# Starting a transform's first stage before the transform ahead of it has ended

## The chip, the cores and the metric

The kernel runs on one core of a Trainium2 chip. The metric is the device time of one execution in microseconds (us), the median of several runs. A core has TensorE (matmuls; PE in the profile, with its weight loads as PEld), VectorE (DVE), ScalarE (ACT), GpSimd (POOL) and SyncE (SP), which only issues DMAs here. Each engine works through its own queue in order.

## The reference

For each of 8 batches of 3008 tokens x 256 channels: a real Fourier transform along the tokens, a product with a filter, the transform back. All 24064 tokens then go through an MLP with a hidden size of 2048. All arrays are float32.

```python
X = np.fft.rfft(x, axis=1)
Y = X * (filt_r + 1j * filt_i)[None]
y = np.fft.irfft(Y, n=S, axis=1)          # (8, 3008, 256)
h = y.reshape(B * S, D) @ w_in            # 256 -> 2048
g = h * (1.0 / (1.0 + np.exp(-1.702 * h)))
out = g @ w_out                           # 2048 -> 256
```

## The kernel before

**The MLP** sets the order of everything. The tokens are cut into 48 tiles (six for each batch) of 512 columns, or 384 for the sixth tile of an even batch. Each tile has 16 **chunks** of 128 hidden units, so the main loop over `turns` has 768 chunks, numbered 0 to 767. A chunk is twelve matmuls: six into `h` (line 784; operands are split into a high and a low part, and three products are kept), ScalarE's Gelu into `gh` (line 787) and again in place (line 788), VectorE's difference `gl` (line 789), and six matmuls into `o` (line 808). From chunk 96 the first half of a chunk is traced two chunks ahead of its second half.

**The transform of a batch** (`fft(b)`) is a generator that the main loop advances by a step now and then. A length of 3008 is split into 64 x 47. From the third batch on (b = 2, `packed`), the **first stage** has 24 steps `transform(n, h)`: POOL's sums and differences of the two halves of `x` (line 519), a split by ScalarE and POOL (lines 525 and 526), one matmul (line 537), a copy by ScalarE and two sums by VectorE (lines 539 to 541), and a store to `a_d` in device memory, issued by ScalarE two steps later (line 468). Four steps that load the first of `x` and prepare the first operands come ahead. The **second stage** has 64 steps (two halves of `forward(i)` and two of `backward(i)`, i from 0 to 15): POOL loads `zy` from `a_d` (line 574), matmuls multiply by the 47-point matrices (lines 585 to 588; those of i = 0 by lines 585 and 586), VectorE and POOL multiply by the filter (lines 596 to 617), and the results go to `b_d`. The tiles' own preparation (`signal`, `turned_signal`) reads `b_d` later.

**When a step is taken** is written out by hand. Each batch but the first has a leg, a list of costs (`COSTS`); the main loop takes the next step when the chunks passed since the leg before have reached its share. Legs follow each other: batch b's first step comes when the last step of batch b - 1 has been taken. A leg ends 18 chunks (12 in one case) ahead of the tile that needs it.

**The order in the queues** is not simply the order of the program. The Tile framework is called with `schedule_with_timeline_sim=True`: it orders each engine's instructions by the times at which it expects their operands. Matmuls marked `keep_in_program_order` (those of the transform among them) keep their order among such instructions.

**Buffers.** In the first stage `x`, the results `a` (two steps to a buffer) and later also `be`, `br` and `zt` share one ring, `raw`, of seven buffers; the split operands, the sums `ev` and the tiles' halves share `half`, of seven. `b_t`, a tile of 24 KB a partition, is used by the first batch alone.

Of the kernel before, what the change touches and what calls it, by code (L numbers as in the profile page):

```python
# [20 lines left out]
P = 128  # L21
Q = 112
NFC = DFF // P
LATER = [0.5, 0.5, 1.0, 0.4] + [0.625, 0.625, 0.375, 0.375] * 15 + [1.0]
COSTS = [[0.746] * 12 + [1.212] * 2 + LATER] + [[0.8] * 4 + [0.675] * 24 + [1.3] * 2 + LATER] * 7

LEAST = 2.0**-15
MOST = float(np.uint32(0x47EFFFFF).view(np.float32))
# [139 lines left out]
def tile_kernel(  # L168
# [19 lines left out]
    def raw(name):  # L188
        return sb.tile([P, 4, D], F32, tag="raw", name=name, bufs=7)
# [270 lines left out]
    def fft(b):  # L460
# [4 lines left out]
        def keep(n=2):  # L465

            for pair in late[:n]:
                nc.scalar.dma_start(*pair)
            del late[:n]

        def thrice():

            for c in range(6):
                xr = raw(f"x_{b}_{c}")
                load_in(xr, x[b, c])
                ah, al = (sb.tile([P, 4, D], F32R, tag="raw", name=f"a{n}_{b}_{c}", bufs=7) for n in "hl")
                for u in range(2):
                    xh, xl = half(f"xh_{b}_{c}_{u}"), half(f"xl_{b}_{c}_{u}")
                    src = xr[:, 2 * u : 2 * u + 2, :]
                    nc.scalar.copy(xh, src)  # L480
                    nc.gpsimd.tensor_tensor(xl, src, xh.bitcast(F32), ALU.subtract)
                    ps = ring("f", [P, 2, D], f"s1_{b}_{c}_{u}")
                    mm3(ps, t1_sb[0][:, 0], t1_sb[0][:, 1], xh, xl)
                    su = slice(2 * u, 2 * u + 2)
                    nc.scalar.copy(ah[:, su], ps)
                    nc.vector.tensor_tensor(al[:, su], ps, ah[:, su].bitcast(F32), ALU.subtract)
                    keep()
                    yield
                for k, a in enumerate((ah, al)):
                    for j in range(2):  # L490
                        n = NH * j + 4 * c
                        pair = (a_d[k][:, n : n + 4], a[64 * j : 64 * j + 64].bitcast(F32))
                        if b == 1:
                            late.append(pair)
                        else:
                            nc.scalar.dma_start(*pair)

        def packed():

            if b == 2:  # L500
                t1_sb.append(const.tile([P, 2, 2, 2, 64], F32R, tag="t1_sb", name="t1_two"))
                t1 = table["t1_s"].rearrange("p (a c) -> p a c", a=2)
                for h in range(2):
                    hi = t1_sb[1][:, h, :, h]
                    nc.scalar.copy(hi, t1)
                    nc.vector.tensor_tensor(t1_sb[1][:, h, :, 1 - h], t1, hi.bitcast(F32), ALU.subtract)
            sides = [(slice(64 * h, 64 * h + 64), slice(64 - 64 * h, P - 64 * h)) for h in range(2)]
            xs, sums, es = {}, {}, {}

            def fetch(c):  # L510
                if c < 6:
                    xs[c] = raw(f"x_{b}_{c}").rearrange("p (j i) d -> p j i d", j=2)
                    load_in(xs[c], x[b, c].rearrange("p (j i) d -> p j i d", j=2))

            def butterfly(n):
                if n < 12:
                    c, j = divmod(n, 2)
                    sums[n] = xs[c][:, 1] if j else sb.tile([P, 2, D], F32, tag="half", name=f"ev_{b}_{c}", bufs=7)
                    nc.gpsimd.tensor_tensor(sums[n], xs[c][:, 0], xs[c][:, 1], ALU.subtract if j else ALU.add)

            def split(n, h):
                if n < 12:
                    src, (t, o) = sums[n], sides[h]
                    es[n, h] = half(f"e{h}_{b}_{n}")
                    nc.scalar.copy(es[n, h][t], src[t])
                    nc.gpsimd.tensor_tensor(es[n, h][o], src[t], es[n, h][t].bitcast(F32), ALU.subtract)

            made = {}

            def transform(n, h):  # L530
                c, j = divmod(n, 2)
                if h == 0:
                    made[n] = sb.tile([P, 2, 2, D], F32, tag="raw", name=f"a_{b}_{n}", bufs=7)
                a, (t, o) = made[n], sides[h]
                ps = ring("f", [P, 2, D], f"s1_{b}_{n}_{h}")
                w = t1_sb[1][:, h, j].rearrange("p a c -> p (a c)")
                tc.keep_in_program_order(nc.tensor.matmul(ps, w, es.pop((n, h)), start=True, stop=True))  # L537
                hi, lo = a[t, 0].bitcast(F32R), a[t, 1]
                nc.scalar.copy(hi, ps[t])  # L539
                nc.vector.tensor_tensor(lo, ps[t], a[t, 0], ALU.subtract)  # L540
                nc.vector.tensor_tensor(lo.bitcast(F32R), lo, ps[o], ALU.add)
                q = NH * j + 4 * c + 2 * h
                late.append((a_d[:, :, q : q + 2].rearrange("k s n d -> s k n d"), a[t]))

            for c in range(2):
                fetch(c)
            for c in range(2):
                yield
            butterfly(0)
            butterfly(1)  # L550
            yield
            for h in range(2):
                split(0, h)
            yield
            for n in range(12):
                for h in range(2):
                    transform(n, h)
                    split(n + 1, h)
                    if h:
                        butterfly(n + 2)  # L560
                        if n % 2 == 0:
                            fetch(n // 2 + 2)
                    if len(late) > 2:
                        keep(1)
                    yield

        yield from packed() if b > 1 else thrice()

        b_d = dram.tile([48, 64, D], F32, tag="b_d", name=f"b_d{b}")

# [5 lines left out]
        def load_f(i):  # L576
            for k in range(2):
                load_in(f_buf[64 * k : 64 * k + 48, 2 * (i % 2) : 2 * (i % 2) + 2], fs[i])
# [54 lines left out]
                        nc.scalar.dma_start(b_d[:, 32 * n + 4 * g : 32 * n + 4 * g + 4, :], be[64 * n : 64 * n + 48])  # L633
                yield

        keep(4)
        if b == 1:
            nc.gpsimd.memset(zy[0].bitcast(F32), 0.0)
        for i in range(2):
            load(i)  # L640
            load_f(i)

        for i in range(2):
            yield
        for i in range(17):
            if i < 16:
                yield from forward(i)
            if i:
                yield from backward(i - 1)
        b_of[b] = b_d  # L650

    def signal(b, t, y):

# [181 lines left out]

    carry = const.tile([P, 2, 2, 64], F32R, tag="carry", name="carry")
    b_t = []
    ys, t2_two, gelu = {}, [], []

    def start(b, t):  # L840
        ys[b, t] = sb.tile([P, 2, 2, 512], F32R, tag="y", name=f"y_{b}_{t}")
# [32 lines left out]
    for j in range(2, len(tiles)):  # L874
# [5 lines left out]
            steps = [NFC * (j - 1) + k for k in at]  # L880
        for n in steps:
            due.setdefault(n, []).append(j)
    legs, passed, since = [], 0, 0
    for b in range(B - 1):
        upto = sum(NFC * width(i) for i in range(6 * b + 6)) - 4 * LEAD - ((18 if b > 1 else 12) * width(6 * b + 5) if b else 26)
        legs.append((COSTS[b], list(COSTS[b]), upto))
    nxt = [fft(1)]
    for n, (i, fc) in enumerate(turns):
        b, t = tiles[i]
        if n == 0:  # L890
            run(start(*tiles[1]))
        if n == 2 * NFC:
            shared[0] = "f"
        if n == 6 * NFC:
            shared[0] = "h"
        while begun <= min(n + 1 + (n >= 6 * NFC), len(turns) - 1):
            ahead(*turns[begun])
            begun += 1
        chunks_of[i][1](fc, turns[n + 1 : n + 2] == [(i, fc + 1)])
        if fc == 1:  # L900
            store()
        if n < 26:
            run(conv, 1)
            if n % 2 and n < 12:
                load_unit(EARLY + 9 + n // 2)
        if n == 11:
            split_de()
            in_order[0] = False
        if n == 26:
            zy.append(const.tile([P, 4, 2, 2, D], F32R, tag="zy", name="zy"))  # L910
        if n >= LEAD and legs:
            passed += width(i)
            costs, steps, upto = legs[0]
            while steps and sum(costs) - sum(steps) + steps[0] <= sum(costs) * (passed - since) / (upto - since) + 0.01:
                run(nxt[0], 1)
                steps.pop(0)
            if not steps:
                legs.pop(0)
                nxt[0] = fft(B - len(legs)) if legs else None
                since = upto  # L920
        for j in due.pop(n, ()):
            if j not in sigs:
                sigs[j] = start(*tiles[j])
            run(sigs[j], 1)
            if not any(j in later for later in due.values()):
                run(sigs[j])
# [29 lines left out]
```

## Time and profile before

| what | value |
|---|---|
| median of 3 runs | 2334.66 us (2334.61 to 2335.33) |
| the profiled execution's own time | 2334.13 us |
| its span, first to last instruction | 2332.3 us |
| busy: TensorE / VectorE / ScalarE / POOL | 100% / 69% / 62% / 48% |
| HBM read and written | 173.80 and 114.82 MB |

The time is taken around the execution; the span is read from the trace of one such execution and lies inside it. Busy is the share of the span in which an engine has an instruction under way; the ends of matmuls are modelled.

### The profile page before, as it was taken

The numbers are of one execution on the slowest core, as the hardware profiler recorded it, in microseconds if no ns is written. First come the engines' busy times: TensorE is split into PE (matmuls) and PEld (weight loads), VectorE is DVE, ScalarE is ACT, GpSimd is POOL, SyncE is SP. The second block draws the span as 40 slices with busy tenths as digits, with TensorE's granted clock in tenths as the row PEclk, the third lists the DMA queues.
The fourth block names the chain that finished last, engine by engine and source line by source line (L and its number), as shares of the span: only waits on it lengthen the run. The fifth ranks groups of instructions, "written<-read, shape, count | busy, mean of one in ns | idle before, by whom it ended". The sixth has DMA issues, their size and how long they took to land.

```text
span 2332.3 us, 32211 instructions
## 1 busy us (share of the span) xinstructions
PE 2324.5 (100%) x10630; PEld 1944.9 (83%) x10630; DVE 1607.8 (69%) x2404; ACT 1439.8 (62%) x2654; POOL 1128.0 (48%) x999
## 2 busy tenths in 40 slices
PE   9999999999999999999999999999999999999999
PEld 7878898888888889888888888988888888888887
DVE  7978866688667885678855887568876688623222
ACT  6666657666675666756676666766657666544443
POOL 3035546466564665556654565736657466311010
PEclk9999999999999999999999999999999999999999
DMA  9265545566455664556545554555655465411100
GB/s 338 82 192 111 111 107 146 134 135 135 109 145 125 144 140 127 154 121 139 127 133 141 133 128 117 153 134 125 138 134 145 118 138 118 101 52 52 57 28 19
DMA packets 189238, 290.75 MB, mean 125 GB/s; under 512 B 18576, under 2 KB 125200, under 8 KB 189072
## 3 DMA queue, kind: packets, MB, share of 16 engines
q1 hardware_dynamic: 112368, 178.20, 26.5%
q0 software_dynamic: 46592, 44.05, 11.4%
q10 hardware_dynamic: 30112, 66.44, 11.1%
q8 instruction: 85, 1.39, 0.3%
q14 instruction: 81, 0.66, 0.1%
HBM read 173.80 MB, written 114.82 MB: 124 GB/s over the span
## 4 chain that ended last, share of the span: by engine, by line
PE 93%; DVE 0%; ACT 0%; issue 0%
PE o L808 42%; PE h L784 42%; PE s L588 2%; PE i L588 2%; PE s L537 1%; PE i L305 1%; PE i L307 1%; PE i L306 1%; PE i L700 0%; PE bt L671 0%; PE s L585 0%; PE s L586 0%; PE i L586 0%; PE i L585 0%; DVE out L816 0%; ACT gh L787 0%
## 5 line engine op out<-in xcount | busy, mean ns | idle before, releaser
L784 PE MATMUL h<-y,wi 128*128 128x512 f32 (+1 forms) x4608 | 1177.3, 385 | 0.1
L784 PEld LDWEIGHTS h<-y,wi 128*128 128x128 f32 x4608 | 858.9, 188 | 165.2 <-DVE gl L789 1.0
L789 DVE TENSOR_TENSOR gl<-h,gh 128x512 fp32r<-128x512 f32 (+1 forms) x768 | 520.7, 678 | 495.4 <-ACT h L788 467.9
L808 PE MATMUL o<-gh,wo 128*128 128x512 f32 (+1 forms) x3072 | 839.2, 385 | 1.2 <-ACT gh L787 1.2
L787 ACT ACTIVATE gh<-h 128x512 fp32r<-128x512 f32 (+1 forms) x768 | 452.2, 589 | 606.6 <-PE h L784 462.9
L808 PEld LDWEIGHTS o<-gh,wo 128*128 128x128 f32 x3072 | 573.4, 188 | 111.6 <-ACT gh L787 1.9
L808 PE MATMUL o<-gl,wo 128*128 128x512 f32 (+1 forms) x1536 | 481.6, 385 | 0.5 <-DVE gl L789 0.5
L788 ACT ACTIVATE h<-h 128x512 f32<-128x512 f32 (+1 forms) x768 | 449.0, 585 | 0.0
L617 POOL TENSOR_TENSOR zy<-c_buf,zy 48x512 fp32r<-48x512 f32 x224 | 316.0, 1411 | 75.0 <-DVE zy L616 63.3
L808 PEld LDWEIGHTS o<-gl,wo 128*128 128x128 f32 x1536 | 287.5, 188 | 56.5 <-DVE gl L789 1.1
L612 POOL TENSOR_TENSOR c_buf<-c_buf,u_buf 112x512 f32<-112x512 f32 x112 | 144.6, 1291 | 229.2 <-DVE c_buf L611 229.2
L574 POOL DMA_DIRECT2D zy<-a_d x224 | 130.3, 586 | 232.5 <-PE s L588 92.9
L740 POOL TENSOR_TENSOR bl<-br,bh 128x512 fp32r<-128x512 f32 x80 | 107.1, 1353 | 246.5 <-ACT bh L739 204.7
L720 POOL TENSOR_TENSOR y<-y 128x512 fp32r<-128x512 f32 (+1 forms) x86 | 105.3, 1230 | 205.2 <-ACT y L719 193.8
L597 DVE TENSOR_TENSOR c_buf<-s,c_buf 48x512 f32<-48x512 f32 x224 | 154.1, 688 | 33.3 <-ACT c_buf L596 28.6
L596 ACT COPY c_buf<-s 48x512 f32<-48x512 f32 x224 | 130.2, 581 | 70.9 <-PE s L588 58.5
L596 ACT COPY b<-i 48x512 f32<-48x512 f32 x224 | 130.1, 581 | 58.4 <-PE i L588 46.5
L597 DVE TENSOR_TENSOR b<-i,b 48x512 f32<-48x512 f32 x224 | 153.8, 687 | 15.1 <-ACT b L596 10.3
L540 DVE TENSOR_TENSOR a<-s,a 64x512 f32<-64x512 f32 x144 | 99.0, 688 | 63.3 <-ACT a L539 60.5
L616 DVE CAST zy<-c_buf 48x512 fp32r<-48x512 f32 x224 | 109.4, 488 | 39.8 <-POOL c_buf L612 34.6
L605 DVE TENSOR_TENSOR u_buf<-c_buf,f_buf 48x512 f32<-48x512 f32 x112 | 110.3, 985 | 3.8
L539 ACT CAST a<-s 64x512 fp32r<-64x512 f32 x144 | 83.7, 581 | 40.8 <-PE s L537 26.6
(126 smaller groups left out, 1789.5 us busy)
## 6 DMA issues: line engine op xcount, KB each, us to landing
f_buf<-fs SPq DMA_DIRECT2D x224, 192.0 KB, 3.4
zy<-a_d POOLq DMA_DIRECT2D x224, 192.0 KB, 3.7
a_d<-a ACTq DMA_DIRECT2D x144, 256.0 KB, 3.0
x<-in_x_dram SPq DMA_DIRECT2D x47, 512.0 KB, 5.5
out_dram<-out SPq DMA_DIRECT2D x43, 512.0 KB, 3.7
b_d<-b ACTq DMA_DIRECT2D x112, 192.0 KB, 2.8
br<-b_d SPq DMA_DIRECT2D x84, 256.0 KB, 4.5
z_d<-zt SPq DMA_DIRECT2D x40, 512.0 KB, 2.7
```

What stands on the lines that cost most here:

```text
L574: nc.gpsimd.dma_start(zy[0][64 * k : 64 * k + 48, i % 2].rearrange("p k s d -> p (k s) d"), src)
L596: nc.scalar.copy(dst[h], ps[o])
L597: nc.vector.tensor_tensor(dst[h], ps[h], dst[h], ALU.add)
L605: nc.vector.tensor_tensor(u2[64:Q], u1[0:48], f_i[0:48], ALU.mult)
L612: nc.gpsimd.tensor_tensor(u1, u1, u2, ALU.add)
L616: nc.vector.tensor_copy(y[h, k], u1[h])
L617: nc.gpsimd.tensor_tensor(y[o, k], u1[h], y[h, k].bitcast(F32), ALU.subtract)
L784: nc.tensor.matmul(ps[:, :w], wi_sb[half][:, wk, kc, c], y[:, yk, kc, :w], start=n == 0, stop=n == 5)
L787: nc.scalar.activation(gh[:, :w], ps[:, :w], AF.Gelu_apprx_sigmoid)
L788: gelu.append(nc.scalar.activation(ps[:, :w], ps[:, :w], AF.Gelu_apprx_sigmoid).ins)
L789: nc.vector.tensor_tensor(gl[:, :w], ps[:, :w], gh[:, :w].bitcast(F32), ALU.subtract)
L808: ins = nc.tensor.matmul(pos[m][:, :w], wb[:, P * m : P * m + P], g[:, :w], start=first_one, stop=last_one)
```

## The change

The generator `fft` becomes a function that returns two generators, the first stage and `two()`, the second. Each step of both gets a time of its own, in sixteenths of a tile's columns passed, and all steps of all batches are sorted into one list. `SPACED` gives, for the third, the fourth and all later batches: how many chunks ahead of the end of the transform in hand the first stage begins (0, 16, 24), how many of its 24 steps lie there (0, 4, 6, one in four chunks), and over how many chunks after that end the others are spread (26, 20, 17). The four preparing steps lie 6, 4.5, 2.2 and 1.1 chunks ahead of the first. The loads of `zy` come 1.5 chunks after the last first-stage step and the first second-stage step 4 chunks after it; the rest of the second stage is spread over what is left, up to the same end as before.

The first stage's buffers become one tile, `s1_pool`, in the memory of `b_t`: three places for `x`, two for the results `a`, and one for two `ev`. The transform of b = 1 (`thrice`) keeps its times.

```diff
-COSTS = [[0.746] * 12 + [1.212] * 2 + LATER] + [[0.8] * 4 + [0.675] * 24 + [1.3] * 2 + LATER] * 7
+SPACED = [(0, 0, 26), (16, 4, 20), (24, 6, 17)]
+FIRST_LEG = [0.746] * 12 + [1.212] * 2 + LATER
...
             if b == 2:
+                s1_pool.append(const.tile([P, 6, 4, D], F32, tag="b_t", name="s1_pool"))
...
-                    xs[c] = raw(f"x_{b}_{c}").rearrange("p (j i) d -> p j i d", j=2)
+                    xs[c] = s1_pool[0][:, c % 3].rearrange("p (j i) d -> p j i d", j=2)
...
-                    sums[n] = xs[c][:, 1] if j else sb.tile([P, 2, D], F32, tag="half", name=f"ev_{b}_{c}", bufs=7)
+                    sums[n] = xs[c][:, 1] if j else s1_pool[0][:, 5, 2 * (c % 2) : 2 * (c % 2) + 2]
...
-                    made[n] = sb.tile([P, 2, 2, D], F32, tag="raw", name=f"a_{b}_{n}", bufs=7)
+                    made[n] = s1_pool[0][:, 3 + n % 2].rearrange("p (k u) d -> p k u d", k=2)
...
-        yield from packed() if b > 1 else thrice()
+        def two():
+            keep(len(late))
...
+            b_of[b] = b_d
...
+        return packed() if b > 1 else thrice(), two()
...
+            early, beside, alone = SPACED[min(b, 4) - 2]
+            first = since - 4 * early
+            last = since + 4 * alone
+            lead = first - 4 * np.array([6.0, 4.5, 2.2, 1.1])
+            one = [*lead, *(first + (since - first) * np.arange(beside) / max(beside, 1))]
+            one += list(since + (last - since) * (np.arange(24 - beside) / (23 - beside)))
+            two = [last + 4 * 1.5, last + 4 * 3, *(last + 4 * 4 + (upto - last - 4 * 4) * np.cumsum([0.0, *LATER[1:]]) / sum(LATER[1:]))]
+        one = [*one, two[0]]
+        steps += [(when, b, which) for which, ats in enumerate((one, two)) for when in ats]
+        since = upto
+    steps.sort()
...
-        if n >= LEAD and legs:
+        if n >= LEAD:
             passed += width(i)
...
+            while steps and steps[0][0] <= passed + 0.01:
+                _, leg, which = steps.pop(0)
+                if leg not in legs:
+                    legs[leg] = fft(leg)
+                run(legs[leg][which], 1)
```

## Rows read from the trace of the kernel before

**Rows 1.** The page: span, and TensorE's busy time, share and instructions

```profile
span 2332.3 us, 32211 instructions
PE 2324.5 (100%) x10630; PEld 1944.9 (83%) x10630; DVE 1607.8 (69%) x2404; ACT 1439.8 (62%) x2654; POOL 1128.0 (48%) x999
```

**Rows 2.** Windows, TensorE alone: stretch, us, busy (matmuls), granted clock, DMA share, GB/s

```profile
0.00:175.00 175.00, 171.58 (x886) 1.00 0.62 204
175.00:2325.00 2150.00, 2150.00 (x9734) 1.00 0.49 118
2325.00:2332.30 7.30, 2.88 (x13) 0.96 0.19 72
```

**Rows 3.** Waits of TensorE: for whom, us in total, times, longest

```profile
PE o L808 <- ACT gh L787: 1.2, 2, 1.0
PE idle L326 <- DVE zero L373: 1.1, 1, 1.1
```

**Rows 4.** Windows: busy (count) of PE, PEld, DVE, ACT, POOL, then clock, DMA

```profile
757.90:816.20 58.30, 58.30 (x259) 48.30 (x258) 52.30 (x78) 37.32 (x68) 35.22 (x34) 1.00 0.68 144
...
2098.80:2157.10 58.30, 58.30 (x259) 48.28 (x258) 17.89 (x26) 26.09 (x48) 7.66 (x6) 1.00 0.17 51
```

**Rows 5.** Waits of ScalarE and POOL, columns as in rows 3

```profile
ACT gh L787 <- PE h L784: 462.9, 455, 4.2
...
POOL zy L574 <- PE s L588: 92.9, 44, 6.0
```

**Rows 6.** Timeline: one Gelu, and the matmuls that read its result

```profile
1560.09 0.60 ACT L787 ACTIVATE gh<-h 128x512 fp32r<-128x512 f32 x1 [1.48 <-PE h L784]
...
1565.78 1.07 PE L808 MATMUL o<-gh,wo 128*128 128x512 f32 x4
```

**Rows 7.** Windows by stage, columns as in rows 4

```profile
709.00:906.00 197.00, 197.00 (x897) 166.05 (x896) 155.53 (x226) 121.71 (x227) 111.19 (x105) 1.00 0.57 129
906.00:988.00 82.00, 82.00 (x384) 70.59 (x383) 54.90 (x82) 59.87 (x112) 51.38 (x40) 1.00 0.57 160
...
334.20:350.90 16.70, 16.70 (x104) 16.70 (x104) 5.54 (x10) 7.72 (x18) 1.08 (x1) 1.00 0.37 87
```

**Rows 8.** Source views of lines 468 and 574: durations in ns, landing times

```profile
L468 ACTq DMA_DIRECT2D a_d<-a x144: 581/582/646, 357.9 to 1836.0; - x144
...
DMA to landing us min/median/max: 2.9/3.1/7.2
...
L574 POOL DMA_DIRECT2D zy<-a_d x224: 574/582/730, 171.6 to 1993.7; - x112
...
DMA to landing us min/median/max: 3.1/3.7/7.1
```

**Rows 9.** Timeline at the fourth batch's handover: start, us, instruction, idle before it

```profile
987.60 0.39 PE L537 MATMUL s<-e,t_two 128*128 128x512 f32 x1
...
990.13 0.58 ACTq L468 DMA_DIRECT2D a_d<-a  x1
...
993.65 2.29 POOL L574 DMA_DIRECT2D zy<-a_d  x4 [16.38 <-DMA a_d<-a]
...
1000.30 0.28 PE L585 MATMUL s<-zy,de_sb 128*128 128x256 f32 x1
...
1000.76 0.28 PE L585 MATMUL s<-zy,de_sb 128*128 128x256 f32 x1
```

**Rows 10.** Timeline at the third batch's handover

```profile
708.26 0.39 PE L537 MATMUL s<-e,t_two 128*128 128x512 f32 x1
...
717.26 2.29 POOL L574 DMA_DIRECT2D zy<-a_d  x4 [16.16 <-issue]
...
721.80 0.19 PEld L585 LDWEIGHTS s<-zy,de_sb 128*128 128x128 f32 x1 [0.21 <-issue]
721.86 0.33 PE L585 MATMUL s<-zy,de_sb 128*128 128x256 f32 x1
```

**Rows 11.** Source view of line 605: durations of one shape, min/median/max in ns

```profile
L605 DVE TENSOR_TENSOR u_buf<-c_buf,f_buf x112: 684/860/1814, 182.2 to 2009.1; 48x512 f32<-48x512 f32 x112
```

More of the change, by code (lines that the diff above doesn't have):

```diff
@@ L565, in packed @@
                     yield
-        yield from packed() if b > 1 else thrice()
+        def two():
+            keep(len(late))
+            if b == 1:
+                nc.gpsimd.memset(zy[0].bitcast(F32), 0.0)
+            for i in range(2):
+                load(i)
+                load_f(i)
+            for i in range(2):
+                yield
+            for i in range(17):
+                if i < 16:
+                    yield from forward(i)
+                if i:
+                    yield from backward(i - 1)
+            b_of[b] = b_d
         b_d = dram.tile([48, 64, D], F32, tag="b_d", name=f"b_d{b}")
@@ L634, in backward @@
                 yield
[L636 to L650, printed above, removed]
+        return packed() if b > 1 else thrice(), two()
     def signal(b, t, y):
@@ L837, in tile_kernel @@
     b_t = []
-    ys, t2_two, gelu = {}, [], []
+    ys, t2_two, gelu, s1_pool = {}, [], [], []
     def start(b, t):
@@ L882, in tile_kernel @@
             due.setdefault(n, []).append(j)
[L883 to L887, printed above, removed]
+    steps, passed, since = [], 0, 0
+    for b in range(1, B):
+        upto = sum(NFC * width(i) for i in range(6 * b)) - 4 * LEAD - ((18 if b > 2 else 12) * width(6 * b - 1) if b > 1 else 26)
+        if b == 1:
+            at = np.cumsum(FIRST_LEG) * (upto / sum(FIRST_LEG))
+            one, two = at[:12], at[12:]
+        else:
+            early, beside, alone = SPACED[min(b, 4) - 2]
[9 more added lines that the diff above has]
+    steps.sort()
+    legs = {}
     for n, (i, fc) in enumerate(turns):
@@ L910, in tile_kernel @@
             zy.append(const.tile([P, 4, 2, 2, D], F32R, tag="zy", name="zy"))
-        if n >= LEAD and legs:
+        if n >= LEAD:
             passed += width(i)
[L913 to L920, printed above, removed]
+            while steps and steps[0][0] <= passed + 0.01:
[3 more added lines that the diff above has]
+                run(legs[leg][which], 1)
         for j in due.pop(n, ()):
```

## The prediction

> **What bounds the kernel now.** I read the page first: the span is 2332.3 us and TensorE is busy for 2324.5 of them [rows 1]. The profiled execution as a whole took 2334.13 us, so 1.8 us lie around the span; the median of the runs shown, 2334.66, is 0.5 us above that execution. Next I cut TensorE's time into three stretches [rows 2]: from 175 to 2325 us it is busy for 2150.00 of 2150.00 us. All its idle time is 3.4 us before 175 (set-up and first transform) and 4.4 us in the last 7.3 (the last outputs). The waits of TensorE say the same: the longest entry is 1.2 us in the whole run [rows 3].
>
> A modelled busy time could hide waiting, so I counted matmuls. The stretch 757.9 to 816.2 lies in a second stage, with the transform's work on every engine; 2098.8 to 2157.1 comes after all transforms. Both hold 259 matmuls in 58.3 us [rows 4], 0.225 us for each, although VectorE is busy for 52.3 us in the first and 17.9 us in the second. The granted clock is 1.00 in both, the level of 2.4 GHz. So TensorE issues at a fixed rate whatever the transform does beside it. A chunk (twelve MLP matmuls) is 12 x 0.225 = 2.70 us. The kernel's time is its number of matmuls times that pace.
>
> What the transform must not do is to make TensorE wait. ScalarE waits for TensorE, not the other way round: 455 of the 768 first Gelus found ScalarE idle until the matmul was done, 462.9 us in total [rows 5]. The Gelu of 1560.09 ends at 1560.69; counting on, the matmuls that read its result are those of 1565.78 [rows 6], 5.1 us later. A delay of ScalarE under some 5 us is not felt there.
>
> **The change part by part.**
>
> *Counts.* No matmul, cast, subtraction or DMA is added or removed: 0 us. One tile of six blocks takes the place of buffers from the shared rings, in memory whose last reader (the first transform's last turn, at chunk 73) lies before its first use at chunk 79. The program of the first transform is the same but for one generator split in two at the same chunk.
>
> *The second stage has more room* (from 58 to 79 chunks for 64 steps: 1.10 to 0.81 steps a chunk, and 0.25 first-stage steps a chunk come in beside it at its end). Any gain would have to come out of TensorE's waiting, and after 175 us there is none that the view shows: 0 us. The most that could be saved at all is the 7.8 us outside the busy time, and the change touches neither end.
>
> *The first stage, 24 steps.* Per step I take the stage 906 to 988 [rows 7] less the load of a stretch with no transform [rows 4], scaled by 82/58.3: ScalarE (59.87 - 36.70)/24 = 0.97 us, VectorE (54.90 - 25.16)/24 = 1.24, POOL (51.38 - 10.77)/24 = 1.69. The steps after the second stage's end came one per 1.17 chunks, now about one per 1.05. With one chunk and one matmul, 2.93 us, for a step, the loads become: ScalarE 45% + 0.97/2.93 = 78%, VectorE 31% + 42% = 73%, POOL 13% + 58% = 71%. Nobody fills up; the cover is the 5 us of [rows 6], the price 0. For the second batch the stage begins 10 chunks earlier, in the narrow tile. In 334 to 351 us, ScalarE is busy 46%, VectorE 33%, POOL 6% [rows 7]; six steps add 5.8, 7.4 and 10.1 us to the 7.7, 5.5 and 1.1 there, below the 16.7 + 1.4 us of the stretch: 0.
>
> *The steps beside the second stage* (four or six, one in four chunks). Their 6 x 1.69 = 10.1 us on POOL stand behind the loads of zy there, which wait at POOL's head for a matmul, up to 6.0 us at a time [rows 5]. A step's operands are split two steps ahead, now eight chunks or 21.6 us, so 6 us don't reach TensorE. The six x loads of a batch go out earlier on SP, past the filter's and the signal's loads; a slot is free four steps before its load, so SP's queue isn't held: 0.
>
> *Slots.* The results of the first stage have two buffers instead of a share of seven. A step writes where the step four before it wrote; that store is issued two steps later, so it has two steps, 5.9 us, to land. Stores land in 3.1 us in the median and 7.2 at most [rows 8]: typically no wait, at worst 1.3 us of ScalarE, with the Gelus behind it, inside the 5 us. Value 0; the other end is a rival below.
>
> *The handover, the only place where something gets tighter.* After the last first-stage matmul: copy and sums, the last store, its landing, the loads of zy by POOL, their landing, then the first second-stage matmul. In the fourth batch the matmul of 987.60 is followed by the last store at 990.13 and four zy loads from 993.65 [rows 9]. The first matmul needs the first two loads: 993.65 + 0.57 + the median landing of 3.7 [rows 8] is 997.9, or 10.3 us after 987.60. In the third batch the loads go out at 717.26 after 708.26 [rows 10], so 13.3 us. Between the two matmuls the program had five or six chunks, and now has four: 4 x 2.70 = 10.8 us. If TensorE came to the matmul exactly there, it would wait 0 us with the fourth batch's chain and 2.5 with the third's: 0 to 6 x 2.5 = 15 us over the six batches that the change touches. Which end? The first two second-stage steps are a chunk or more apart in the program, yet their matmuls stand at 1000.30 and 1000.76 [rows 9]. The order of the queue isn't the program's: the first one was put behind MLP matmuls, 12.7 us after 987.60, some 2.4 us after its data. The same placing would let MLP matmuls go ahead when only four chunks are given. The third batch shows the edge: the weight load of 721.80 stood idle for 0.21 us, and the matmul began at 721.86 [rows 10]. I take the near end: 0.2 us for all six.
>
> Sum: 2334.13 + 0 + 0.2 = 2334.3 for an execution like the profiled one, and with the median's 0.5 us, 2334.9 us.
>
> **The rivals.** A measurement of this kernel can tell about 0.2%, 4.7 us, from no change.
>
> *The handover is waited for* (slower). For it: four chunks are about as long as the chain, and the third batch already touches it. Against: the placing just described. Price up to 15 us, 2349.9 us; it decides from 0.8 us a batch. Chance 0.06.
>
> *Two result buffers bind* (slower). If the halves of a buffer, which lie in different partitions, are held as one, a step waits for the store issued only one step before: landing 3.1, issue 0.58 and 0.5 us from landing to the next instruction [rows 8, 9] make 4.2 us a step against 2.93. Over 20 steps in six batches that is 120 x 1.3 = 156 us, less the 5 us of cover in each: 2461 us. Even half of it would show. Against: nothing says that they are held as one, and at two steps the median store lands in time. Chance 0.03.
>
> *VectorE or POOL becomes the bound while the stages run side by side* (slower). For it: the product of line 605, which reads two SBUF operands, takes from 684 to 1814 ns for one shape [rows 11], so something blocks it at times. Against: VectorE has (197 - 155.53)/197 = 21% idle in a second stage [rows 7], 13.6 us in 24 chunks, and POOL's added work is 10.1 us. It decides only if all of that and 3.5 us more were blocked. If twice the added work were blocked, the four batches with 24 chunks would lose 4 x 6.6 = 26 us: 2361 us. Chance 0.03. The Trainium skill, "SBUF — State Buffer", section "Who interferes with whom", says that a VectorE instruction with two SBUF inputs contends with a GpSimd instruction that reads SBUF and that the later one is blocked for the whole of the other. By that rule each added POOL operation can cost VectorE its full duration, an estimate of 10 us a batch, which speaks against this change; the spread of [rows 11] agrees with it.
>
> *TensorE has room after all* (faster). If a thinner second stage let matmuls issue closer together, a 0.3% shorter pitch would be enough: 2150 x 0.003 = 6.5 us, 2328.4 us. Against: 259 in 58.3 us with the transform and without [rows 4]. Chance 0.02. The Trainium skill, "TensorE: Matmul & The Clock Gate", section "Back-to-back issue gap", gives about 131 ns for a sustained matmul of 512 columns in a stream of weight loads and matmuls; by that, TensorE would not be the bound and the time could fall by far more. The rows have 225 ns at every load, so the trace disagrees, and no run here shows the lower figure.
>
> **How the numbers follow.** The forecast, no measurable change, holds 0.86; its own range is 2333.6 to 2337. Slower is 0.06 + 0.03 + 0.03 = 0.12, faster 0.02. The low end, 2333.4, is no gain with a slightly quicker median; the high end, 2340, takes in the handover's wait up to 0.9 us a batch; some one in ten lies above it and a few in a hundred below.
>
> **What the changed profile would show.** TensorE busy for all of 175 to 2325 us, still 259 matmuls of full width in 58.3 us, and no entry above some 1 us in its waits. First-stage matmuls of the next batch among second-stage ones, every 11 us; a second stage of some 228 us from its first matmul to its last (79 x 2.70 and 66 x 0.225). At each handover the first matmul within 0.5 us or more after its zy loads. A prediction too low would show as TensorE waiting on zy's DMA at six places, or as ScalarE's copy of line 539 waiting for a_d stores and Gelus late behind it.

## The result: 0.55% slower, lost in 78 us of the run

The changed kernel takes 2347.71 us in the median (2346.73 to 2349.37, 4 runs) against 2334.99 for the kernel before: a ratio of 1.0055, 95% interval 1.0038 to 1.0072. The forecast was 2334.9 us in 2333.4 to 2340.0, with 0.86 on no measurable change: wrong. The profiled execution took 2347.43 us. Its span and its engines' busy times:

```profile
span 2345.7 us, 32023 instructions
PE 2328.7 (99%) x10630; PEld 1945.4 (83%) x10630; DVE 1625.6 (69%) x2404; ACT 1440.7 (61%) x2654; POOL 1141.0 (49%) x999
```

The span has grown by 13.4 us [rows 1]; TensorE's idle time (span less busy) by 9.2, from 7.8 to 17.0 us, and its busy time, for the same 10630 matmuls, by 4.2. The windows of TensorE say where (stretch, us, busy and matmuls, granted clock, DMA share, GB/s):

```profile
175.00:285.00 110.00, 110.00 (x519) 1.00 0.56 121
285.00:335.00 50.00, 45.97 (x216) 1.00 0.41 100
335.00:363.00 28.00, 24.15 (x134) 0.94 0.45 127
363.00:2338.00 1975.00, 1974.20 (x8869) 1.00 0.49 118
```

Where [rows 2] had no gap, 7.9 us of idle time now lie between 285 and 363 us, the meeting of the second batch's second stage with the third batch's first. From 363 to 2338 us, with the five later meetings and all their steps side by side, there is 0.8 us. The waits of TensorE, beside [rows 3]:

```profile
PE i L704 <- DMA br<-b_d: 3.9, 1, 3.9
PE h L788 <- DVE gl L793: 2.3, 2, 1.5
PE o L812 <- ACT gh L791: 2.0, 4, 1.0
PE i L606 <- POOL zy L635: 0.9, 1, 0.9
```

Lines have moved: 788, 791, 793 and 812 are the MLP's first matmul, Gelu, difference and second matmul; 521 and 528 POOL's sums and split differences; 606 a second-stage matmul; 634 VectorE's cast of its product; 704 the first matmul of a tile's preparation, which reads `br`.

The pace of TensorE where it doesn't wait is that of [rows 4], here in a stage with two batches side by side:

```profile
771.20:829.50 58.30, 58.30 (x259) 48.31 (x258) 47.78 (x69) 38.23 (x69) 43.00 (x38) 1.00 0.70 139
```

**What happens between 285 and 363 us.** POOL's groups from 285 to 345 us (count, busy, mean ns), first of the changed kernel, then of the kernel before:

```profile
L635 POOL TENSOR_TENSOR zy<-c_buf,zy 48x512 fp32r<-48x512 f32 x10 | 13.8, 1381 | 4.5 <-DVE zy L634 3.9
L528 POOL TENSOR_TENSOR e<-s_pool,e 64x512 fp32r<-64x512 f32 x8 | 11.6, 1445 | 3.9 <-ACT e L527 3.5
L521 POOL TENSOR_TENSOR s_pool<-s_pool 128x512 f32<-128x512 f32 x8 | 10.3, 1298 | 4.0 <-DMA s_pool<-in_x_dram 3.6
```

```profile
L617 POOL TENSOR_TENSOR zy<-c_buf,zy 48x512 fp32r<-48x512 f32 x10 | 13.9, 1393 | 3.9 <-DVE zy L616 3.5
...
L526 POOL TENSOR_TENSOR e<-ev,e 64x512 fp32r<-64x512 f32 x2 | 2.6, 1284 | 0.2
L519 POOL TENSOR_TENSOR ev<-x 128x512 f32<-128x512 f32 x1 | 1.3, 1293 | 0.0
L519 POOL TENSOR_TENSOR x<-x 128x512 f32<-128x512 f32 x1 | 1.3, 1288 | 0.1
```

The third batch's share of POOL went from 4 operations (5.2 us) to 16 (21.9 us), beside the same ten subtractions of the second batch. VectorE's groups from 285 to 305 us, changed kernel, then before:

```profile
L634 DVE CAST zy<-c_buf 48x512 fp32r<-48x512 f32 x2 | 2.9, 1455 | 0.0
L629 DVE TENSOR_TENSOR c_buf<-c_buf,f_buf 112x512 f32<-112x512 f32 x2 | 2.6, 1281 | 0.0
L615 DVE TENSOR_TENSOR c_buf<-s,c_buf 48x512 f32<-48x512 f32 x3 | 2.1, 690 | 3.5 <-ACT c_buf L614 3.4
```

```profile
L597 DVE TENSOR_TENSOR c_buf<-s,c_buf 48x512 f32<-48x512 f32 x5 | 3.5, 691 | 1.0 <-ACT c_buf L596 0.9
...
L616 DVE CAST zy<-c_buf 48x512 fp32r<-48x512 f32 x4 | 1.7, 416 | 0.1
L611 DVE TENSOR_TENSOR c_buf<-c_buf,f_buf 112x512 f32<-112x512 f32 x2 | 1.4, 687 | 0.0
```

One shape takes 1455 ns instead of 416, another 1281 instead of 687; the sum with one operand in PSUM keeps its 690. The timeline shows how this reaches TensorE (start, us, instruction, idle before it):

```profile
285.62 1.27 ACT L527 CAST e<-s_pool 64x512 fp32r<-64x512 f32 x2 [2.26 <-POOL s_pool L521]
...
287.50 0.60 ACT L791 ACTIVATE gh<-h 128x512 fp32r<-128x512 f32 x1
...
288.16 1.19 PE L812 MATMUL o<-gh,wo 128*128 128x512 f32 x4 [0.31 <-ACT gh L791]
...
300.33 2.94 DVE L634 CAST zy<-c_buf 48x512 fp32r<-48x512 f32 x2
...
303.78 0.68 DVE L793 TENSOR_TENSOR gl<-h,gh 128x512 fp32r<-128x512 f32 x1
...
304.51 0.73 PE L788 MATMUL h<-y,wi 128*128 128x512 f32 x2 [1.50 <-DVE gl L793]
```

The same chunk's Gelu and matmuls in the kernel before (the 71st of each, counted from the start):

```profile
284.54 0.61 ACT L787 ACTIVATE gh<-h 128x512 fp32r<-128x512 f32 x1
...
287.65 1.07 PE L808 MATMUL o<-gh,wo 128*128 128x512 f32 x4
```

There the cover was 285.15 to 287.65, 2.5 us, and not the 5 us that [rows 6] has at 1560 us. In the changed kernel the Gelu starts 3.0 us later: ahead of it in ScalarE's queue stood the third batch's splits, which waited 2.26 us for POOL's first sum. So it ends at 288.10, and TensorE waits. The difference `gl` of 303.78 had to let two slow casts pass. Last, SP's queue, changed kernel and before:

```profile
279.22 1.83 SPq L209 DMA_DIRECT2D s_pool<-in_x_dram  x3
...
351.12 3.25 SPq L209 DMA_DIRECT2D br<-b_d  x4
```

```profile
318.46 1.44 SPq L208 DMA_DIRECT2D x<-in_x_dram  x2
...
337.02 2.65 SPq L208 DMA_DIRECT2D br<-b_d  x4
```

The third batch's `x` is fetched 39 us sooner, and the second batch's result 14 us later: its second stage ends late, and its last store lands late (run 11). That is the wait of 3.9 us at 354 us. After it the granted clock falls from 2.4 GHz to its other level, 1.2 GHz:

```profile
354.00:358.00 4.00, 0.63 (x4) 1.00 1.03 296
358.00:360.00 2.00, 1.51 (x12) 0.91 0.17 45
360.00:362.00 2.00, 2.00 (x10) 0.50 0.00 0
362.00:364.00 2.00, 2.00 (x10) 0.74 0.59 131
```

By these rows 2 x 0.09 + 2 x 0.50 + 2 x 0.26 = 1.7 us of the 4.2 us of longer busy time are the clock's; the rest, matmuls drawn out around the waits, was not taken apart.

### The profile page after: what moved, and what is told of

The parts are those of the page before. It is cut to its first block, busy times and chain, and to the rows that moved or that the text cites. A ratio compares the mean times of both kernels' runs of the same rounds, so it can differ in the third digit from the quotient of the medians.

```text
span 2345.7 us, 32023 instructions
## 1 busy us (share of the span) xinstructions
PE 2328.7 (99%) x10630; PEld 1945.4 (83%) x10630; DVE 1625.6 (69%) x2404; ACT 1440.7 (61%) x2654; POOL 1141.0 (49%) x999
## 4 chain that ended last, share of the span: by engine, by line
PE 90%; DVE 1%; DMA 1%; ACT 0%; issue 0%; POOL 0%; SPq 0%; ACTq 0%; POOLq 0%; DVEq 0%
PE o L812 41%; PE h L788 41%; PE s L606 2%; PE i L606 2%; PE s L539 1%; PE i L306 1%; PE i L308 1%; PE i L307 1%; PE i L704 0%; DMA br<-b_d 0%; DVE gl L793 0%; DMA s_pool<-in_x_dram 0%; DVE zy L634 0%; DVE s_pool L542 0%; DVE b L615 0%
## 5 line engine op out<-in xcount | busy, mean ns | idle before, releaser
L528 POOL TENSOR_TENSOR e<-s_pool,e 64x512 fp32r<-64x512 f32 x144 | 193.1, 1341 | 43.0 <-ACT e L527 24.6
L634 DVE CAST zy<-c_buf 48x512 fp32r<-48x512 f32 x224 | 126.0, 563 | 24.6 <-POOL c_buf L630 18.4
L542 DVE TENSOR_TENSOR s_pool<-s,s_pool 64x512 f32<-64x512 f32 x144 | 98.8, 686 | 35.4 <-ACT s_pool L541 33.0
L541 ACT CAST s_pool<-s 64x512 fp32r<-64x512 f32 x144 | 83.7, 581 | 42.8 <-PE s L539 33.8
```

Source lines behind the costliest of these rows:

```text
L634: nc.vector.tensor_copy(y[h, k], u1[h])
```

## The experiments

Theory A: the loss is the third batch's preparation, pulled into the second batch's dense second stage. Rivals: B, the first stage's own few buffers; C, the later batches' handovers. Each number is a median beside that of the kernel before on the same chip, with the ratio's interval.

**1. The third batch back to its old times.**

```diff
+        elif b == 2:
+            at = since + np.cumsum(OLD) * ((upto - since) / sum(OLD))   # OLD: the costs before
+            one, two = at[:28], at[28:]
```

> Only the third batch gets its old step times back; the six-block tile and the new times of the later batches stay. Theory A (all of the loss comes from the third batch's first stage starting 10 chunks earlier, beside the second batch's dense second stage): 2335 us, within 1.5 us of the kernel before, and TensorE never idle between 285 and 363 us. Theory B (the loss comes from the first stage's own few buffers): 2345 us or more. Theory C (the loss is spread over the handovers of the later batches): 2342 us or more.

2338.23 against 2334.78 us: 1.0015 (1.0006 to 1.0024). Of 12.7 us, 3.4 are left, more than A had room for. TensorE's windows show no idle time behind 335 us, so C falls:

```profile
285.00:335.00 50.00, 48.66 (x235) 1.00 0.40 94
335.00:363.00 28.00, 28.00 (x157) 1.00 0.34 82
363.00:2328.00 1965.00, 1965.00 (x8828) 1.00 0.49 119
```

**2. All later batches back to their old times**, the third not (`elif b > 2`).

> The complement: only the third batch keeps its new step times, all later batches get the old ones; the six-block tile stays. Theory A: the whole loss is still there, 2346 to 2349 us, with TensorE idle for some 8 us between 285 and 363 us. Theory B: 2345 us or more as well. Theory C: 2336 us or less.

2346.86 against 2334.78: 1.0051 (1.0036 to 1.0066). Nearly the whole loss stays, as A has it; B isn't excluded by this run.

**3. All new times, the old rings of buffers** (`raw` and `half` for `x`, `ev` and the results).

> All new step times, but x, ev and the results come from the shared rings of seven buffers as before. Theory A in its plain form (the times alone do it): 2345 us or more. Theory B (the own buffers do it, by letting the loads and POOL's sums run ahead of their place or by making the copies wait): 2335 to 2337 us.

2348.70 against 2334.78: 1.0061 (1.0046 to 1.0076). B as the whole cause falls: without the tile the loss is no smaller. But part of it lies elsewhere; of TensorE's windows, the last:

```profile
363.00:2340.00 1977.00, 1971.88 (x8850) 1.00 0.48 118
```

Behind 363 us there are 5.1 us of waits that the kernel with the tile has not (0.8). In these runs the tile is what lets the later batches work side by side without cost.

**4. The tile alone**, all old times (`elif b > 1`).

> All old step times, with the six-block tile of the change. Theory A: 2335 us, within 1.5 us of the kernel before. Theory B: 2340 us or more.

2338.14 against 2334.78: 1.0015 (1.0006 to 1.0025). The tile costs 3.4 us by itself, between the two expectations. With runs 1 and 2: the tile 3.4, the later batches' new times 0.1 (2338.23 - 2338.14), the third batch's new times 8.7 (2346.86 - 2338.14); together 12.2 of 12.7 us.

**5. Two chunks of cover from chunk 64 on** instead of 96.

```diff
-        if n == 6 * NFC:
+        if n == 4 * NFC:
             shared[0] = "h"
-        while begun <= min(n + 1 + (n >= 6 * NFC), len(turns) - 1):
+        while begun <= min(n + 1 + (n >= 4 * NFC), len(turns) - 1):
```

> The changed kernel, but the first half of a chunk is traced two chunks ahead from chunk 64 on instead of chunk 96 (and the spare PSUM bank goes to it then). Theory A1 (the third batch's early work hurts because TensorE has only one chunk of cover before chunk 96): the waits of 287 to 333 us shrink from 4 us to under 1, and the time falls to 2336 to 2343 us; the wait for br may stay, since it hangs on the second stage's end. Rival A2 (the cover doesn't matter, the second stage as a whole is late): 2346 us or more.

2351.93 against 2334.95: 1.0075 (1.0060 to 1.0090). Slower: A1 falls as stated. Two things changed at once, so the run doesn't say what the cover alone is worth: the waits of 287 to 303 us go, but the ring of the transform loses a PSUM bank to the MLP, and the waits move to the second stage and to what needs its end:

```profile
PE i L704 <- DMA br<-b_d: 7.2, 1, 7.2
PE s L606 <- DVE b L615: 2.5, 2, 2.3
```

**6. The third batch 14 chunks later.**

```diff
-SPACED = [(0, 0, 26), (16, 4, 20), (24, 6, 17)]
+SPACED = [(-14, 0, 40), (16, 4, 20), (24, 6, 17)]
...
-            one += list(since + (last - since) * ...)
+            begin = max(since, first)
+            one += list(begin + (last - begin) * ...)
```

> The changed kernel, but the third batch's first stage starts 14 chunks after the second batch's second stage has ended instead of with its end, its 24 steps over 26 chunks as before. Theory A (work of the third batch pulled into the dense second stage): no wait of TensorE over 0.5 us between 285 and 363 us, 2335 to 2336.5 us. Rival (a shorter second stage for the third batch, 46 chunks, costs as much elsewhere): 2340 us or more, with waits between 450 and 650 us.

2361.78 against 2334.95: 1.0116 (1.0100 to 1.0131). Both are seen:

```profile
285.00:335.00 50.00, 49.97 (x247) 1.00 0.46 103
...
585.00:680.00 95.00, 79.80 (x309) 0.86 0.58 150
```

The stretch in question is whole again, which is A; but the third batch's second stage, left 46 chunks, meets the fourth batch's early first stage, and 15.2 us of idle time come there, with a mean clock of 0.86. Most of the waits are for sums that VectorE has late, one meeting later.

**7. As run 1, with the third batch's `x` from the old ring.**

```diff
-xs[c] = s1_pool[0][:, c % 3].rearrange("p (j i) d -> p j i d", j=2)
+xs[c] = (raw(f"x_{b}_{c}") if b == 2 else s1_pool[0][:, c % 3]).rearrange("p (j i) d -> p j i d", j=2)
```

> As the run in which the third batch has its old times, but the third batch's x also comes from the old ring of seven, so that its first loads wait for a free buffer. Theory P (the 3.4 us that the own tile costs with old times come from x loads that no buffer holds back, 40 us sooner, and POOL's sums right behind them): x loads after 315 us, no waits at 287 to 303 us, 2334.5 to 2335.5 us. Rival (the tile costs in another way, by the two result buffers): still 2337.5 us or more.

2335.60 against 2334.95: 1.0004 (0.9994 to 1.0013), no difference that can be told. So the tile's 3.4 us hang on the third batch's `x` loads, which no busy buffer held back any more, with POOL's sums right behind them; theory P holds. The loads alone cost nothing that can be told: in this run too three `x` loads go into the tile at 281.06 us (by the code a later batch's), but POOL's first sum comes at 328.53. This is also the changed kernel without its loss: all later batches have the new times and the tile, and the time is that of the kernel before, not less.

**8. The second batch's casts on ScalarE.**

```diff
-                nc.vector.tensor_copy(y[h, k], u1[h])
+                (nc.scalar.copy if b == 1 else nc.vector.tensor_copy)(y[h, k], u1[h])
```

> The changed kernel, but in the second batch's second stage the two casts of each step (line 634) run on ScalarE instead of VectorE. Theory V (VectorE's casts are held up by POOL's work on the third batch, 1.46 us each instead of 0.42, and the Gelu difference behind them is late): the waits of TensorE for line 793's differences (1.5 and 0.8 us) go, and the time falls by 2 to 4 us, to 2344 to 2346 us. Rival Q (POOL's queue itself is what is late): no fall, or a rise by ScalarE's load, 2347 us or more.

2349.22 against 2334.95: 1.0062 (1.0045 to 1.0079). Inconclusive: the wait of 302 us went, but with 32 casts more on ScalarE there were other waits (2.7 us for differences in all, the longest 1.6), 3.1 us for `br` stayed, and the time did not fall.

**9. The third batch 5 chunks later** (`(-5, 0, 31)`, otherwise as run 6).

> The changed kernel, but the third batch's first stage starts 5 chunks later than in the change, its 24 steps over 26 chunks as there; its second stage is left 59 chunks, about what it had before. Theory A (the closer the third batch's preparation lies to the end of the second batch's second stage, the longer both wait): the wait for br and the waits of 318 to 335 us go or shrink to under 2 us in all, the 3 us of the unheld x loads stay, 2337 to 2341 us. Rival (as in the run with 14 chunks, a later first stage only moves the cost to the meeting with the fourth batch): waits between 590 and 675 us, 2345 us or more.

2344.47 against 2335.10: 1.0039 (1.0024 to 1.0054). Between the expectations: nothing is lost behind 363 us, 0.6 us between 335 and 363, but 4.4 us between 285 and 335. The changed kernel lost 4.0 us between 285 and 335, so five chunks later don't relieve that stretch; what shrank is the wait for `br`, from 3.9 to 0.6 us.

**10. The third batch's sums and split differences on VectorE** (`nc.vector if b == 2 else nc.gpsimd` in lines 521 and 528).

> The changed kernel, but the third batch's sums and split differences (lines 521 and 528) run on VectorE instead of POOL; its times and buffers are those of the change. Theory Q (POOL's queue is what the second batch's second stage waits for): POOL has no third-batch work between 285 and 345 us, the second stage ends by 336 us instead of 343, no wait for br, 2335 to 2341 us. Rival V (VectorE is the scarce engine there): Gelu differences late, 2348 us or more.

2345.51 against 2335.10: 1.0044 (1.0029 to 1.0059). Neither theory: the wait for `br` is gone, as Q has it, but the second batch's last store is issued at 343.66 us, 9 us later than in the kernel before, and not by 336. A difference `gl` is waited for 3.6 us; VectorE has ten of the moved operations between 285 and 295 us. Neither engine has room there, and how much of the late end is POOL's queue this run can't say.

**11. All new times, the third batch's `x` from the old ring** (the edit of run 7 alone).

> The changed kernel with all its times, but the third batch's x from the old ring of seven. Theory (two separate costs, the unheld x loads and the earlier steps): the waits of 287 to 303 us go, those of 318 to 363 us stay with the wait for br, 2343 to 2348 us. Rival (the unheld loads are the whole cause): 2335 to 2337 us.

2342.17 against 2335.10: 1.0031 (1.0020 to 1.0041), just below the range of the two-cost theory, far from the rival. The two costs aren't simply added: the old ring saves 5.6 us here (12.7 - 7.1) and 2.8 with the third batch's old times (3.45 - 0.65, runs 1 and 7). The waits of 287 to 303 us are gone, and so is the one for `br`, which was expected to stay. In the changed kernel the second batch's last store is issued just behind an `x` load:

```profile
345.75 0.35 SPq L209 DMA_DIRECT2D s_pool<-in_x_dram  x1
...
346.07 0.55 ACTq L651 DMA_DIRECT2D b_d<-b  x1
```

It landed 4.9 us after its issue, and the second `br` load, which the matmuls need too, after 6.5. In run 11 no `x` load stands there; the last store went out at 345.19 and landed after 2.4 us, and that `br` load after 4.0. Runs 2 and 8 have the order of the changed kernel, and a wait for `br` of 3.1 us each; runs 3, 9, 10 and 12 have not, and wait 0.6 us or less. No run moved this load alone, so its part is argued, not shown. One long wait is left:

```profile
325.85 1.60 POOL L528 TENSOR_TENSOR e<-s_pool,e 64x512 fp32r<-64x512 f32 x1
...
326.35 2.78 DVE L634 CAST zy<-c_buf 48x512 fp32r<-48x512 f32 x2
327.52 1.33 POOL L528 TENSOR_TENSOR e<-x,e 64x512 fp32r<-64x512 f32 x1
...
329.16 0.56 DVE L793 TENSOR_TENSOR gl<-h,gh 128x384 fp32r<-128x384 f32 x1
...
329.77 1.65 PE L788 MATMUL h<-y,wi 128*128 128x384 f32 x4 [3.29 <-DVE gl L793]
```

Two casts last as long as POOL's two operations, to within 0.3 us (329.13 and 328.85); the difference queued behind them comes at once, and TensorE after it.

**12. Run 11 with the last four steps' casts on ScalarE** (the edit of run 8 with `b == 1 and i >= 12`).

> The run before (all new times, the third batch's x from the old ring), but in the last four steps of the second batch's second stage the casts of line 634 run on ScalarE. In the run before TensorE's one long wait, 3.3 us at 326 us, stood behind two casts of 1.39 us each (0.42 alone), while POOL had one third-batch operation after the other. Theory V (VectorE's casts are held by POOL's operations and the Gelu difference queued behind them is late): that wait falls under 0.5 us, 2335 to 2339 us. Rival Q (POOL's queue makes the second stage late, whoever casts): a wait of 2 us or more stays between 310 and 363 us, 2341 us or more.

2337.38 against 2334.79: 1.0013 (1.0004 to 1.0022), 2.6 us above the kernel before, where run 11 is 7.1 above. The wait for differences is 0.5 us in the whole run, and ScalarE's new load costs 1.2:

```profile
PE o L812 <- ACT out L819: 1.2, 1, 1.2
...
PE h L788 <- DVE gl L793: 0.5, 1, 0.5
```

Theory V holds for this wait: POOL's work was there in both runs, and only the casts were taken out of its way.

## Why the prediction was wrong, point by point

*What bounds the kernel, and that nothing can be won:* right. TensorE's pace is unchanged, and run 7, the change without its loss, is at the time of the kernel before. The Trainium skill's 131 ns a matmul ("TensorE: Matmul & The Clock Gate", section "Back-to-back issue gap") is not seen here either: it is 259 in 58.3 us again, 225 ns. The second stage was taken a little too long: the 79 chunks count the four of the handover too, and from its first matmul to its last it took 207 to 222 us in the four batches concerned (969.36 to 1176.4 in the fifth), not 228. Nothing else hangs on that.

*"For the second batch the stage begins 10 chunks earlier, in the narrow tile"*, priced 0 (it is b = 2, the third batch counted from one), is the step that failed. It priced six transforms in the light stretch of 334 to 351 us, and had no term for the four preparing steps, which the change puts 6 to 1.1 chunks ahead of the second batch's end. Nor is a step's place in the program its place in a queue. The preparation ran from 284 us on, under the second batch's second stage, where POOL had 12 operations more than before. It also used the 5 us of cover of [rows 6], read at 1560 us, where TensorE is two chunks ahead; before chunk 96 it is one ahead, and at 285 us the kernel before has 2.5 us between a Gelu and its matmuls. Priced 0; the third batch's new times cost 8.7 us.

*"One tile of six blocks takes the place of buffers from the shared rings"*, priced 0 as well, failed too, by 3.4 us: the ring of seven had held the `x` loads back until 318 us. That hold was useful, and the tile took it away (runs 4 and 7). The last read of `b_t` starts at 278.9 us, and the loads follow at 279.22; chunk 79, where the program has them, runs at about 318 us, by the count of line 812's matmuls.

*The rival "VectorE or POOL becomes the bound while the stages run side by side"* (0.03) was the right mechanism in the wrong place: it was priced for the four batches with 24 chunks, where run 1 shows nothing. It struck at the one meeting with a dense second stage and little cover. The price per engine, idle time against added work, missed that one late operation at the head of ScalarE's or VectorE's queue is enough. The Trainium skill, "SBUF — State Buffer", section "Who interferes with whom", has a VectorE instruction with two SBUF inputs contend with a GpSimd instruction that reads SBUF, and a copy or cast in a two-port mode with GpSimd; the later of the two is blocked for the whole of the other. An instruction with at most one SBUF input, outside such a mode, is untouched. The trace agrees: 1455 ns against 416 for the casts, 1281 against 687 for the product with two SBUF inputs, 690 against 691 for the sums that read PSUM.

*The handover*: right. No entry of the waits names the first second-stage matmuls, and behind 363 us TensorE loses 0.8 us. *The two result buffers*: right, no copy of line 541 waits for a store.

Not settled: how much of the second stage's late end is POOL's queue, what the `x` load ahead of its last store does by itself, and how the remaining 2.6 us of run 12 divide. That the early place in the queues comes from the framework's expected times is argued from the order in the traces, not tried.

## What to carry to other kernels

Price a moved step where its instructions land in the queues, and look there for the cover that its neighbours have; the cover of another stage proves nothing. A shared ring that is full is also a brake: give a stage buffers of its own, and its loads and everything behind them start as soon as the queues let them. Here one engine was full from end to end, so a change of order had nothing to win; it lost where two dense stages met.

## What the runs showed of the hardware

At two places a wait of TensorE cost more than its length. After idle stretches of 3.3 us (run 11) and 3.9 us the granted clock read 0.50, the level of 1.2 GHz, for some microseconds. In run 11:

```profile
330.00:332.00 2.00, 2.00 (x7) 0.50 0.21 41
332.00:334.00 2.00, 2.00 (x8) 0.50 0.83 219
334.00:336.00 2.00, 2.00 (x8) 0.56 0.54 207
```

That is 2 x 0.50 + 2 x 0.50 + 2 x 0.44 = 2.9 us lost after the wait, an estimate from these rows and about as much as the wait itself. With the wait it makes 6.2 of the 7.1 us that run 11 loses.
